# A block mask made from a 24-column one-hot, and expert rows loaded sooner, in a fused attention and mixture-of-experts kernel

## The chip, the cores and the metric

The kernel runs on one core of one Trainium2 chip. Its time is device microseconds, and before the change the median of 3 runs was 718.14 us (717.37 to 718.94). The core has five engines that run side by side, each through its own list of instructions in order, and wait for each other by semaphores: TensorE (PE, matrix products; PEld is its loading of weights), VectorE (DVE), ScalarE (ACT), GpSimd (POOL) and SyncE (SP, which here only issues transfers). An instruction that waits holds up everything behind it on its own engine.

## The reference

Block-sparse attention (BigBird's mask) over 4 batches, 8 heads, 768 positions and 64 dimensions is followed by a mixture of 8 experts, to each of which a token is sent by the cosine of its row with the expert's embedding. Cut to what matters here:

```python
mask = np.abs(blk_i - blk_j) <= 1                       # blocks of 32 positions, 24 of them
mask = mask | (blk_i == 0) | (blk_j == 0) | (blk_i == 23) | (blk_j == 23)
for qb in range(24):
    for kb in sampled_blocks[qb]:                       # 3 random blocks for each
        mask[qb*32:(qb+1)*32, kb*32:(kb+1)*32] = True
scores = np.where(mask, q @ k.T / 8, -1e9)
attn = softmax(scores) @ v                              # for each batch and head
x = heads side by side                                  # 3072 tokens of 512
xn, en = x / |x|, expert_emb / |expert_emb|
expert = argmax(xn @ en.T / tau); gate = softmax(...)[expert]
out[token] = gate * (relu(x[token] @ w1[expert]) @ w2[expert])
```

## The kernel before

The mask is added inside the score products. A key in block n has a one-hot row `kmask` (1 in row n), a query has a column `qmask` (0 where its block may see block n, -1e9 where not), and the product of the two, accumulated into the same PSUM tile as q·k, masks the scores. `kmask` and `qmask` are built once, at the start, from the 24x24 block mask `m`:

```python
def block_mask(k, exact=False):
    dif = iota(k, "dif", [NB, NB], [[1, NB]], mult=-1)          # column - row, on POOL
    col = iota(...); row = iota(...)
    m = dif * dif;  m = m <= 1.5                                # DVE, 24x24
    for val in (0.0, float(NB - 1)):
        for pos in (col, row):
            ins = nc.vector.scalar_tensor_tensor(out=m, in0=pos, scalar=val, in1=m, op0=ALU.is_equal, op1=ALU.max)
    with k.tc.issue_after(ins.ins):
        nc.vector.tensor_copy(out=ids_f, in_=k.ids[:, :, 0])    # the sampled blocks
    for r in range(NRAND):
        nc.vector.scalar_tensor_tensor(out=m, in0=col, scalar=ids_f[:, r:r + 1], in1=m, op0=ALU.is_equal, op1=ALU.max)
    nc.gpsimd.memset(both, 0.0)
    ins = nc.vector.tensor_scalar(out=both[:, :, 0:NB], in0=m..., scalar1=1.0, scalar2=-NEG, ...)
    k.mask_rows = ins.ins
    return both

def build_mask(k):
    nc.vector.memset(k.kmask[0:D], 1.0)                         # 64 x 768
    both = block_mask(k)
    one = k.kmask[0:D]
    nc.gpsimd.affine_select(out=one, in_=one, pattern=[[1, S]], compare_op=ALU.is_ge, fill=0.0, base=0, channel_multiplier=-BLK)
    nc.gpsimd.affine_select(out=one, in_=one, pattern=[[-1, S]], compare_op=ALU.is_ge, fill=0.0, base=BLK - 1, channel_multiplier=BLK)
    nc.scalar.copy(out=k.kmask[D:P], in_=k.kmask[0:D])          # the second head's 64 rows
    ps = k.big.tile([P, 2, 512], F32, name="qr", tag="big")
    for i in range(2):                                          # spread the mask over 768 queries
        cols = slice(i * HALF, (i + 1) * HALF)
        nc.tensor.matmul(ps[:, i, 0:HALF], lhsT=both..., rhs=k.kmask[0:NB, cols], start=True, stop=True)
    for i, copy in enumerate((nc.vector.tensor_copy, nc.scalar.copy)):
        k.masked.append(copy(out=k.qmask[:, cols of half i], in_=ps[:, i, 0:HALF]).ins)
```

The queries and keys of the first pair of heads come as two halves (`part` 0 and 1), are turned by DVE in 32x32 blocks (`kt`, `qt`), and then a unit of work is 128 keys against 384 queries for two heads. There are 192 units, 12 for a pair of heads. Each is scored, exponentiated by ACT, summed by DVE (`esum`), and multiplied with v (`av`). After every six units `av` is copied to `at`, and a few units later `settle` sends it back through TensorE (`back`), with the normed expert rows as further columns, which needs `build_experts` to be done.

```python
def warm_up(k, times):                                          # products of zeros
    ...
    ps = k.acc.tile([P, 2, 512], F32, name="warm", tag="av")
    for i in range(times):
        k.nc.tensor.matmul(ps[:, 0], lhsT=k.zeros[:, 0:P], rhs=k.zeros, start=True, stop=True)

def build_experts(k):                                           # a generator: yields cut it into steps
    nc.scalar.activation(sq, emb, ACT.Square, accum_out=nrm)
    nc.gpsimd.tensor_tensor(out=nrm, in0=nrm, in1=k.half[0:E, 0:1], op=ALU.pow)
    ...; yield
    nrm = (nrm + 1e-6) * tau; nrm = 1 / nrm; emb = emb * nrm     # three DVE operations
    yield
    for c in range(ND):
        nc.tensor.transpose(tp[:, c * E:(c + 1) * E], emb[:, c * P:(c + 1) * P], k.ident[0:E, 0:E])
    ...; yield

def attention_fast(n, ctx):
    load_ids(n); load_blocks(n, 0, 0); load_pair(n, 0, (2,)); load_blocks(n, 0, 1)
    warm_up(n, 8)
    build_mask(n)
    for part, behind in enumerate((n.mask_rows, n.masked[0])):
        with n.tc.issue_after(behind):
            for i in range(2):
                turn_blocks(n, 0, i, part)
    build_ident(n); score_fast(n, 0); score_fast(n, 1); build_consts(n)
    load_blocks(n, 1)                                           # the next pair's k and q
    load_pair(n, 1, (2,))                                       # its v
    load_experts(n)                                             # expert rows and tau
    for u in range(units):
        ...
        if u in (2, 4, 7): next(experts)                        # a step of build_experts
        steps = [attend_fast(u), score_fast(u + 2)]             # the other way round at the first of six units
```

The score products, the mask first (`score_fast`):

```python
    for rows, cols, first in ((k.kmask, k.qmask, True), (kt, qt, False)):
        for h, r, keys in quarters:
            nc.tensor.matmul(ps[D * r:D * (r + 1), h, 0:HALF], lhsT=rows[D * h:D * (h + 1), keys],
                             rhs=cols[D * h:D * (h + 1), queries], start=first, stop=not first)
    k.exps = nc.scalar.activation(e, ps[:, :, 0:HALF], ACT.Exp, scale=SCALE)
```

The score tiles and the spread share two PSUM buffers (`big`), `av` and the warm-up tile one (`acc`). The instructions are ordered by a scheduler when the program is built, and `issue_after` keeps one behind another on its engine. The second half of the kernel, the experts' products, is not touched by the change.

## Time and profile before

| | before |
|---|---|
| median of 3 runs | 718.14 us |
| span of the profiled run | 719.4 us |
| TensorE busy | 698.3 us (97%), 8308 products |
| DVE busy | 335.0 us (47%) |
| GpSimd busy | 229.0 us (32%) |
| ACT busy | 188.5 us (26%) |

Attention takes about the first half of the span and the experts the second. The page divides the span into 40 slices and gives for each the busy tenths of every engine and the clock that TensorE was granted, in tenths of full speed. The chain of waits, followed back from the last instruction, lies 87% on TensorE and 4% on DVE. In the lists of groups and in the timeline, a line gives the start and length in us, the engine, the line of the kernel, the operation, the tiles it writes and reads with their shape, and in square brackets how long its engine had been idle before it and who ended that. PE intervals are modelled, so a busy TensorE need not be at its peak.

### The profile page before, as it was taken

How to read it: one execution, taken by the hardware profiler on the slowest of the kernel's cores; microseconds unless marked ns; L12 is line 12 of the kernel's file. 1: busy time of each engine (PE TensorE's matmuls, PEld its weight loads, DVE VectorE, ACT ScalarE, POOL GpSimd, SP SyncE). 2: the span in 40 equal slices, each digit the busy share in tenths (PEclk: the TensorE clock that was granted, in tenths of full speed). 3: DMA queues.
4: the chain of work that ended last, by engine and by line, in shares of the span. 5: the costliest groups of instructions: out<-in, count | busy, mean ns of one | idle time of the engine just before them, and what ended most of it. 6: DMA issues, size and time to landing. Idle time of an engine off the chain costs nothing.

```text
span 719.4 us, 19421 instructions
## 1 busy us (share of the span) xinstructions
PE 698.3 (97%) x8308; PEld 447.8 (62%) x8308; DVE 335.0 (47%) x683; ACT 188.5 (26%) x266; POOL 229.0 (32%) x385
## 2 busy tenths in 40 slices
PE   7899999999999999999999999999999999999992
PEld 3585555555555455556777677766576665767771
DVE  6677778777788888776582111111111111111110
ACT  4355554454545544554100000000000000000000
POOL 2225547554754547653601111111111121111110
PEclk9899999999999999999999999999999999999997
DMA  6433333365335947642999998998899998999980
GB/s 111 91 67 69 69 68 68 64 154 113 52 69 126 181 99 224 201 136 82 328 316 400 397 337 325 342 338 303 297 396 398 398 347 305 404 397 401 340 321 23
DMA packets 180808, 164.76 MB, mean 229 GB/s; under 512 B 128284, under 2 KB 128284, under 8 KB 180710
## 3 DMA queue, kind: packets, MB, share of 16 engines
q1 hardware_dynamic: 174950, 149.80, 66.6%
q0 software_dynamic: 4160, 13.39, 4.7%
q8 instruction: 69, 1.13, 0.7%
q10 hardware_dynamic: 1600, 0.20, 0.2%
q14 instruction: 29, 0.24, 0.1%
HBM read 147.62 MB, written 16.01 MB: 227 GB/s over the span
## 4 chain that ended last, share of the span: by engine, by line
PE 87%; DVE 4%; issue 3%; POOL 1%; DMA 1%; ACT 1%; SPq 1%; DVEq 0%; POOLq 0%; ACTq 0%
PE hp L840 21%; PE yp L853 21%; PE sc L353 19%; PE av L374 16%; PE back L409 3%; PE hp L881 2%; PE yp L901 2%; PE back L402 1%; PE xg_ps L825 1%; ACT e L356 1%; DVE kt L269 1%; DVE esum L371 1%; DVE at L380 0%; DMA out_dram<-y,slot_l 0%; DMA kld<-in_k_dram 0%
## 5 line engine op out<-in xcount | busy, mean ns | idle before, releaser
L356 ACT ACTIVATE e<-sc 128x768 f32<-128x768 f32 x192 | 155.7, 811 | 161.5 <-PE sc L353 156.3
L840 PEld LDWEIGHTS hp<-xgt,w 128*128 128x128 f32 x1472 | 167.7, 192 | 10.8 <-issue 10.2
L840 PE MATMUL hp<-xgt,w 128*128 128x128 f32 x1472 | 169.1, 275 | 0.0
L353 PE MATMUL sc<-qt,kt 64*64 64x384 f32 x1536 | 167.6, 489 | 0.0
L374 PE MATMUL av<-e,vld 64*64 64x384 f32 x1536 | 162.1, 491 | 2.3 <-DVE at L380 2.0
L853 PE MATMUL yp<-w,h 128*128 128x512 f32 x368 | 162.0, 593 | 0.1
L371 DVE TENSOR_TENSOR esum<-esum,e 128x768 f32<-128x768 f32 x128 | 130.9, 1023 | 44.0 <-ACT e L356 42.2
L853 PEld LDWEIGHTS yp<-w,h 128*128 128x128 f32 x368 | 68.0, 190 | 77.5 <-issue 76.3
L437 POOL TENSOR_TENSOR sq<-sq 128x192 f32<-128x192 f32 (+1 forms) x186 | 103.2, 555 | 13.9
L862 POOL DMA_INDIRECT out_dram<-y,slot_l x20 | 20.2, 1009 | 246.0 <-DVE y L861 233.9
L374 PEld LDWEIGHTS av<-e,vld 64*64 64x64 f32 x1536 | 58.6, 134 | 58.7 <-issue 26.7
L843 ACT ACTIVATE h<-hp 128x512 f32<-128x512 f32 x23 | 13.7, 597 | 298.3 <-PE hp L840 284.4
L353 PEld LDWEIGHTS sc<-qt,kt 64*64 64x64 f32 x1536 | 64.7, 135 | 37.3 <-issue 34.2
L861 DVE TENSOR_SCALAR y<-yp,xg 128x512 f32<-128x512 f32 x25 | 18.8, 750 | 140.7 <-PE yp L853 128.2
L847 DVE TENSOR_SCALAR h<-hp 128x512 f32<-128x512 f32 x23 | 15.9, 691 | 131.3 <-PE hp L840 131.3
L353 PE MATMUL sc<-qmask,kmask 64*64 64x384 bf16 x768 | 71.6, 327 | 1.0 <-DVE qmask L167 1.0
L433 POOL TENSOR_TENSOR sq<-x 128x384 f32<-128x384 f32 x31 | 27.0, 873 | 121.7 <-DVE part L422 108.5
L353 PEld LDWEIGHTS <-kmask 64*64 64x64 bf16 x768 | 27.9, 108 | 32.2 <-issue 31.3
L369 DVE TENSOR_TENSOR esum<-e 128x768 f32<-128x768 f32 x32 | 31.1, 973 | 11.5 <-ACT e L356 10.8
L409 PE MATMUL back<-ones,esum 64*64 64x1 f32 x1536 | 27.5, 192 | 0.0
L409 PEld LDWEIGHTS back<-ones,esum 64*64 64x64 f32 x1536 | 26.6, 137 | 0.0
L780 POOL DMA_INDIRECT xg<-x_dram,slot_l x22 | 22.6, 1026 | 6.7 <-issue 6.7
(193 smaller groups left out, 364.1 us busy)
## 6 DMA issues: line engine op xcount, KB each, us to landing
w<-in_moe_w_dram SPq DMA_DIRECT2D x54, 2048.0 KB
w<-in_moe_w_dram SPq DMA_DIRECT2D x16, 512.0 KB
x_dram<-x SPq DMA_DIRECT2D x24, 256.5 KB
vld<-in_v_dram SPq DMA_DIRECT2D x32, 192.0 KB
kld<-in_k_dram SPq DMA_DIRECT2D x60, 96.0 KB
qld<-in_q_dram SPq DMA_DIRECT2D x60, 96.0 KB
x_early<-x SPq DMA_DIRECT2D x12, 256.5 KB
ticks<-dens SPq DMA_DIRECT2D x32, 0.0 KB
```

The costliest lines, as they stand in the source:

```text
L353: nc.tensor.matmul(ps[D * r:D * (r + 1), h, 0:HALF], lhsT=rows[D * h:D * (h + 1), keys], rhs=cols[D * h:D * (h + 1), queries], start=first ...
L356: k.exps = nc.scalar.activation(e, ps[:, :, 0:HALF], ACT.Exp, scale=SCALE)
L369: k.summed = nc.vector.tensor_tensor(out=k.esum, in0=k.first, in1=e, op=ALU.add)
L371: k.summed = nc.vector.tensor_tensor(out=k.esum, in0=k.esum, in1=e, op=ALU.add)
L374: nc.tensor.matmul(k.av[D * h:D * (h + 1), r, 0:HALF], lhsT=v[D * r:D * (r + 1), h, kc, :], rhs=e[D * r:D * (r + 1), h, :], start=(kc == 0 ...
L409: nc.tensor.matmul(sums[D * s:D * (s + 1), t, h, r:r + 1], lhsT=esum[D * r:D * (r + 1), h, cols], rhs=k.ones[D * r:D * (r + 1), 0:1], star ...
L433: nc.gpsimd.tensor_tensor(out=sq, in0=x, in1=x, op=ALU.mult)
L437: k.squared = nc.gpsimd.tensor_tensor(out=out, in0=sq[:, :, 0:width], in1=sq[:, :, width:2 * width], op=ALU.add).ins
L780: k.nc.gpsimd.indirect_dma_start(out=x[:, :], out_offset=None, in_=(k.x_dram if late else k.x_early)[:, :], in_offset=bass.IndirectOffsetO ...
L840: nc.tensor.matmul(hp[:, f, :], lhsT=w1[:, d, (f0 + f) * P:(f0 + f + 1) * P], rhs=xt[:, d, :], start=(d == 0), stop=(d == ND - 1))
L853: nc.tensor.matmul(yp, lhsT=h[:, f, :], rhs=w2[:, f, :], start=(f == 0), stop=(f == NF - 1))
L862: nc.gpsimd.indirect_dma_start(out=k.out[:, :], out_offset=bass.IndirectOffsetOnAxis(ap=slot, axis=0), in_=y[:, :], in_offset=None, bounds ...
```

## The change

The one-hot rows of `kmask` repeat each block's column 32 times. The change makes them in 24 columns (`hot`, 128x24) with two small DVE comparisons, and lets the readers repeat each column by a stride of zero: ACT's copy into `kmask`, now for both heads at once, and the two products that spread the mask over the queries. The 64x768 memset and the two 64x768 selects are not needed then. The two halves of `qmask` are copied apart: the first by ACT, the second by DVE, behind the turns of the first halves of k and q. Five more products of zeros are placed between the spread and the first scores, to keep TensorE at work there. The expert rows and tau are loaded ahead of the second pair's blocks and not behind them, so that `build_experts` can be ordered sooner.

```diff
@@ warm_up
-    ps = k.acc.tile([P, 2, 512], F32, name="warm", tag="av")
+        k.warm = k.acc.tile([P, 2, 512], F32, name="warm", tag="av")     # made once, with the zeros
     for i in range(times):
-        k.nc.tensor.matmul(ps[:, 0], ...)
+        k.nc.tensor.matmul(k.warm[:, 0], ...)
@@ block_mask
-    dif = iota(k, "dif", [NB, NB], [[1, NB]], mult=-1)
+    lanes = iota(k, "dif", [P, NB], [[1, NB]], mult=-1)
+    dif = lanes[0:NB]
...
+        k.hot = pool.tile([P, NB], BF16, name="hot")
+        for h in range(2):
+            rows = slice(D * h, D * (h + 1))
+            ins = nc.vector.tensor_scalar(out=k.hot[rows], in0=lanes[rows], scalar1=-float(D * h), scalar2=None,
+                                          op0=ALU.is_equal)
@@ build_mask
-    nc.vector.memset(k.kmask[0:D], 1.0)
-    one = k.kmask[0:D]
-    nc.gpsimd.affine_select(...)                                         # twice
-    nc.scalar.copy(out=k.kmask[D:P], in_=k.kmask[0:D])
+    nc.scalar.copy(out=k.kmask.rearrange("p (n t) -> p n t", t=BLK), in_=k.hot.unsqueeze(2).broadcast_to([P, NB, BLK]))
     for i in range(2):
-        nc.tensor.matmul(ps[:, i, 0:HALF], lhsT=both..., rhs=k.kmask[0:NB, cols], ...)
+        some = k.hot[0:NB, i * (NB // 2):(i + 1) * (NB // 2)]
+        k.spread = nc.tensor.matmul(k.qr[:, i, 0:HALF], lhsT=both...,
+                                    rhs=some.unsqueeze(2).broadcast_to([NB, NB // 2, BLK]), start=True, stop=True).ins
-    for i, copy in enumerate((nc.vector.tensor_copy, nc.scalar.copy)): ...
+    mask_half(k, 0, nc.scalar.copy)
@@ attention_fast
     build_mask(n)
-    for part, behind in enumerate((n.mask_rows, n.masked[0])):
-        with n.tc.issue_after(behind):
+    with n.tc.issue_after(n.spread):
+        warm_up(n, 5)
+    for part in range(2):
+        with n.tc.issue_after(n.masked[1] if part else n.mask_rows):
             for i in range(2):
                 turn_blocks(n, 0, i, part)
+        if part == 0:
+            with n.tc.issue_after(n.turns):
+                mask_half(n, 1, n.nc.vector.tensor_copy)
...
+    load_experts(n)
     load_blocks(n, 1)
     load_pair(n, 1, (2,))
-    load_experts(n)
```

As built, the order of the engines changes only at the start: the steps of `build_experts` come on ACT behind the exponential of unit 3 (before: of unit 9), and the four small transposes of the expert rows on TensorE lie between the attention products of units 6 and 7 (before: among the scores of unit 10).

## The prediction

> **What bounds the kernel now.** I read the table of engines first: TensorE is busy for 698.3 of 719.4 us. Then the granted clock by stretch, which I cut at the places where the clock changes:
>
> ```profile
> 0.00:10.83 10.83, 7.05 (x38) 3.05 (x42) 6.97 (x23) 3.40 (x4) 4.24 (x20) 0.84 0.67 118
> 10.83:24.48 13.65, 13.37 (x180) 6.64 (x172) 10.52 (x16) 8.20 (x12) 0.00 (x0) 1.00 0.76 139
> 24.48:27.90 3.42, 1.42 (x32) 0.97 (x34) 1.83 (x7) 0.23 (x2) 0.75 (x1) 1.00 0.73 117
> 27.90:34.72 6.82, 6.82 (x104) 5.65 (x100) 3.12 (x7) 1.46 (x2) 3.40 (x7) 0.50 0.02 5
> 34.72:300.00 265.28, 263.29 (x5042) 151.94 (x5038) 209.73 (x414) 137.23 (x187) 143.73 (x254) 1.00 0.50 105
> ```
>
> After the stretch and its length, the columns are PE, weight loads, DVE, ACT, POOL, clock, DMA share, GB/s. From 34.72 us on TensorE is never free for long and its clock is full. So only the first 35 us can give anything, and what they give should arrive whole at the end: the later weight loads are triggered by work that moves with it. Two places stand out: the opening, with a half clock from 7.41 to 10.83, and 24.48 to 34.72, where TensorE idles and then runs 6.82 us at 0.50.
>
> The timeline of the opening, by engine, shows why scores begin at 7.52:
>
> ```profile
> 1.30 0.70 DVE L152 MEMSET kmask<- 64x768 bf16 x1
> 2.06 0.88 DVE L127 TENSOR_SCALAR m<-m 24x24 f32<-24x24 f32 x1
> 2.08 0.85 POOL L155 TENSOR_SCALAR_AFFINE_SELECT kmask<-kmask 64x768 bf16<-64x768 bf16 x1 [0.67 <-DVE m L126]
> 3.05 0.82 POOL L157 TENSOR_SCALAR_AFFINE_SELECT kmask<-kmask 64x768 bf16<-64x768 bf16 x1
> 3.07 0.83 DVE L130 SCALAR_TENSOR_TENSOR m<-col,m 24x24 f32<-24x24 f32 x1
> 4.00 0.17 DVE L130 SCALAR_TENSOR_TENSOR m<-row,m 24x24 f32<-24x24 f32 x1
> ...
> 5.78 0.17 DVE L140 TENSOR_SCALAR both<-m 24x48 bf16<-24x48 f32 x1
> 5.98 0.58 DVE L269 STREAM_TRANSPOSE kt<-kld 128x384 f32<-128x384 f32 x1
> 6.49 0.54 DVE L269 STREAM_TRANSPOSE qt<-qld 128x384 f32<-128x384 f32 x1
> 6.95 0.52 DVE L167 CAST qmask<-qr 128x384 bf16<-128x384 f32 x1
> 7.50 0.48 ACT L167 CAST qmask<-qr 128x384 bf16<-128x384 f32 x1 [2.57 <-DVE qmask L167]
> 7.52 0.54 PE L353 MATMUL sc<-qmask,kmask 64*64 64x384 bf16 x4 [1.01 <-DVE qmask L167]
> ```
>
> The same 24x24 operation takes 0.83 us beside an affine_select of POOL and 0.17 us afterwards. The DVE chain memset, mask, two transposes, copy is what ends last. The eight warm-up products end at 4.49; TensorE then works 0.49 us until 7.52, and the first 24 score products run in 3.46 us.
>
> The chain of the expert rows, from the timeline around 24 us:
>
> ```profile
> 23.84 0.61 ACT L214 ACTIVATE emb_sq<-emb 8x512 f32<-8x512 f32 x1
> 24.37 0.18 ACT L214 ACTIVATION_READ_ACCUMULATOR emb_sq<-emb 8x1 f32 x1
> 24.64 0.75 POOL L215 TENSOR_TENSOR emb_nrm<-emb_nrm,half 8x1 f32<-8x1 f32 x1 [19.00 <-ACT emb_sq L214]
> 25.42 0.20 DVE L220 TENSOR_SCALAR emb_nrm<-emb_nrm,tau 8x1 f32<-8x1 f32 x1 [0.48 <-DMA qld<-in_q_dram]
> 25.66 0.15 DVE L221 RECIPROCAL emb_nrm<-emb_nrm 8x1 f32<-8x1 f32 x1
> 25.90 0.47 DVE L222 TENSOR_SCALAR emb<-emb,emb_nrm 8x512 f32<-8x512 f32 x1
> 26.52 0.38 PE L226 MATMUL tp<-ident,emb 8*128 8x8 f32 x4 [2.00 <-DVE emb L222]
> ```
>
> The bracket of the last line is the reading: TensorE stood for 2.00 us because the transposes of the expert rows lie in its order in the middle of unit 10's scores, while ACT, POOL and DVE were only then making them.
>
> [...] the changes stand at 7.41, 10.83, 27.90 and 34.72, multiples of 3.41 apart, and each half-clock stretch follows a window in which TensorE was mostly idle (4.00 to 7.41; 24.48 to 27.90, busy 1.42 of 3.42). [...] the trace's copy of kmask took 0.83 us with 64 lanes, so my estimate for the new copy over 128 lanes is the same 0.83.
>
> **The change, part by part.**
>
> (a) One-hot. Out go the 0.70 us memset and both POOL selects; in come two DVE operations on 64x24. The largest like them, `both`, took 0.17, so 0.1 to 0.17 each. The DVE order of the changed kernel is zeros, m, hot twice, m, ids_f, four m, three m, both. It starts when the iota is there (1.07, so about 1.25) instead of 1.92, and loses the two blocked operations (0.88 and 0.83 become about 0.17 each). It is at ids_f by about 1.8, which now precedes the four L130 operations and must wait for the ids transfer; the trace's landings have it complete at 2.21. From the start of the second L130 operation to the end of `both` the old trace has 4.00 to 5.95 = 1.95; plus 0.2 for the first, 2.15. So `both` ends near 2.25 + 2.15 = 4.4, at worst 4.7 if the two 128x128 selects of POOL (0.29 and 0.31) still hit it. Before: 5.95. Gain 1.3 to 1.5 us, but not all on the path:
>
> (b) The transposes. The four k transfers of the first half are unchanged, and their last landing is at 5.25 in the old trace. So kt can start at 5.3 rather than 5.98, and qt ends near 6.4. Half of the gain of (a) is swallowed here.
>
> (c) The halves of the mask. Half 0 goes to ACT: table load to 4.08, kmask copy to 4.9, then the qmask copy of 0.48, about 5.5. It no longer stands behind the transposes on DVE, where it cost 0.45 (7.02 to 7.47). Half 1 stays on DVE after the turns, ending near 7.0; unit 1 needs that only because its score buffer is the one that held the spread, and unit 1 comes at about 7.3. So the first q·k products can start at 6.45 instead of 7.79.
>
> (d) Warm-up. Five more products after the spread (about 4.5 to 5.0). The old ones follow each other at 0.43 us before 4.00, at half clock; at full clock I take 0.21, so 1.07 in all, ending near 6.1, before qt. The window 4.00 to 7.41 is then almost fully busy and the next one should be at full clock. The first 24 score products took 3.46 us at 0.50; the later units do 12 in 1.19 (0.35 + 0.84), so 24 in about 2.4. Unit 2's scores end near 9.4 instead of 11.74: 2.3 us earlier.
>
> (e) What is left of this at the next gate. DVE must copy `at` of the first half before unit 6 can attend: old start 20.13. Now the expert chain comes before: esum of unit 3 near 12.1 to 13.1, POOL's power to about 13.65, then 0.97 for the three expert operations, two esum, two kt transposes (1.03), the back copies (0.55): `at` starts near 18.2, TensorE resumes near 18.8 instead of 20.74. It would have been ready at about 17.8, so it idles about 1 us. **Gain carried: 1.9 us.**
>
> (f) Expert rows. Their load is issued at about 8.7 instead of 17.85, ahead of pair 1's blocks, so it lands near 11.5 if it takes the old 2.75 (17.85 to the last landing at 20.60). ACT squares them after unit 3, and the transposes on TensorE are placed in unit 6's attention (about 19 us), 4 us after the rows are ready. **2.0 us of idle go**, and with them the half clock: 6.82 us at 0.50 did the work of 3.41 at 1.00, **3.4 us more**. Pair 1's k blocks are issued about 0.4 us later (9.5 instead of 9.11) and are read only at about 16.7: no cost.
>
> Sum: 1.9 + 2.0 + 3.4 = 7.3. A cross-check: from `at` to `at` is 16.27 us for the first pair (20.13 to 36.40), and 10.24 for a later one (46.19 to 56.43), a surplus of 6.03, which with 1.9 makes 7.9. I take 7.7: 718.14 - 7.7 = 710.4.
>
> **Rivals.** First, loads bind the opening: (b) is already that in part. If k's first half lands later than 5.25, or q's, the mask's gain vanishes and warm-up becomes filler; what remains is the clock of (d). For it: DVE waited 0.49 us on kld at 8.51 for the second half. Total gain then near 6.5, time 711.6. Second, the warm-up itself delays: if the window's phase leaves the five products at half clock they take 2.15 us and end at 7.1, 0.7 after qt. Part of it is hidden behind (e)'s gate; 711 to 711.5. Third, DVE becomes the bound: the expert chain sits in front of esum, transposes and `at`, and DVE's wait for POOL is dead time. If `at` comes only at 19.5, the start's gain falls to 0.6 and the time is about 711.8; if the idle also makes a cold window, 713.5. Fourth, the cold stretch at 28 us is due to the many one-column products of the first `back` (1.6 us of them there), not to the idle. Against it: later pairs have the same products at clock 1.00 up to 300 us. If it held, only 2.0 + 1.9 would come: 714.2.
>
> **Range and chances.** All four rivals end between 710 and 714.2, and none makes the kernel slower: everything added is 1.07 us of TensorE in otherwise idle time and two short DVE operations. A surplus of 0.5 us over the cross-check gives 709.7; runs of before scatter by 1.6. So 708.7 to 713.3. Two per cent faster would be 703.8, which takes twice the sum; 2% slower has no source.
>
> **What would show it.** Right: POOL without 64x768 selects, `both` done by 4.7; first q·k products at 6.3 to 6.6, granted clock 1.00 from 4.0 through 40; `at` at 18 to 18.5 with an idle of about 1 us before unit 6; no wait of `tp` on DVE; second `at` near 28.3 instead of 36.40. Wrong: a half-clock stretch anywhere in 7 to 40 us, an idle over 2 us before unit 6, or a first product later than 7.

## The result, and the profile after

| | before | after |
|---|---|---|
| median of 6 runs each, side by side | 719.13 us (717.37 to 719.61) | 712.15 us (711.12 to 713.08) |
| ratio, with its 95% interval | 1 | 0.9907 (0.9893 to 0.9922) |
| span of the profiled run | 719.4 us | 711.0 us |
| mean granted clock of TensorE | 0.987 | 0.994 |
| TensorE busy | 698.3 us | 693.6 us |

The kernel became faster: the two medians lie 6.98 us apart, and the ratio makes the gain 0.93%, or 6.7 us. The mean clock of 0.994 still holds the last 8.5 us of the span (from 702.5), which are at 0.50 and in which TensorE has nothing to do; what lay before the first clock record of the trace is counted in it as full clock. The prediction was 710.4 us, with a range from 708.7 to 713.3.

First the windows of the kernel after, with the columns as before: PE, weight loads, DVE, ACT and POOL busy (with counts), clock, DMA share, GB/s.

```profile
2.85:6.26 3.41, 3.41 (x9) 0.86 (x8) 2.29 (x9) 2.54 (x3) 0.47 (x1) 1.00 1.07 204
...
7.06:19.39 12.33, 11.53 (x158) 6.04 (x157) 8.80 (x17) 8.07 (x12) 0.75 (x1) 1.00 0.82 146
19.39:30.00 10.61, 10.61 (x200) 5.92 (x204) 8.55 (x18) 4.64 (x8) 2.94 (x5) 1.00 0.58 94
30.00:40.00 10.00, 10.00 (x200) 5.65 (x196) 8.44 (x15) 5.45 (x8) 4.95 (x8) 1.00 0.62 108
```

From 19.39 us on TensorE is busy in every hundredth of the window, at clock 1.00. Neither the idle 2.00 us nor the half-clock stretch of 6.82 us is there any more. Only the first row misleads: the clock column shows 1.00 until the trace has its first clock record, and that record comes at 6.26 in this run. What ran before it is told by the products themselves.

The timeline of the opening, by engine (start, length, engine, line, operation, tiles; in brackets the idle time before it and who ended it):

```profile
1.20 0.57 DVE L137 TENSOR_SCALAR hot<-dif 64x24 bf16<-64x24 f32 x2
1.25 3.60 PE L80 MATMUL warm<-zeros 128*128 128x512 bf16 x8 [1.25 <-DVE zeros L77]
...
4.14 0.18 DVE L148 TENSOR_SCALAR both<-m 24x48 bf16<-24x48 f32 x1
4.78 0.82 PE L165 MATMUL qr<-hot,both 24*128 24x384 bf16 x2
5.17 0.58 DVE L274 STREAM_TRANSPOSE kt<-kld 128x384 f32<-128x384 f32 x1 [0.86 <-DMA kld<-in_k_dram]
5.53 1.59 PE L80 MATMUL warm<-zeros 128*128 128x512 bf16 x5
5.64 0.48 ACT L172 CAST qmask<-qr 128x384 bf16<-128x384 f32 x1 [0.71 <-PE qr L165]
5.68 0.54 DVE L274 STREAM_TRANSPOSE qt<-qld 128x384 f32<-128x384 f32 x1
...
7.06 0.36 PE L358 MATMUL sc<-qmask,kmask 64*64 64x384 bf16 x4
7.24 0.81 PE L358 MATMUL sc<-qt,kt 64*64 64x384 f32 x8
```

The mask rows are ready at 4.32 instead of 5.95, and the transposes are then held by the landing of k (0.86 us of DVE waiting on a DMA). But the first score product waits for neither of them: `qt` is done at 6.22, the mask's first half at 6.12, and TensorE goes on with its products of zeros until about 7.1. Three things add up there, all before the full clock came at 6.26. The eight products of zeros ran at half clock (3.60 us, 0.45 each) and ended at 4.85, so that the spread began at 4.78, 0.46 us after the mask rows were ready; the two spread products took 0.82; and the five products took 1.59, since the first two of them began before 6.26 as well. A later run of the same kernel, shown below, has 0.50 for the spread and 1.25 for the five, 0.25 each, at full clock.

The expert rows in the timeline of the kernel after, and the two `at` copies that the prediction names:

```profile
12.87 0.61 ACT L219 ACTIVATE emb_sq<-emb 8x512 f32<-8x512 f32 x1
...
14.92 0.47 DVE L227 TENSOR_SCALAR emb<-emb,emb_nrm 8x512 f32<-8x512 f32 x1
18.77 0.56 DVE L385 TENSOR_TENSOR at<-av,part 128x384 f32<-128x384 f32 x1
19.39 0.88 PE L379 MATMUL av<-e,vld 64*64 64x384 f32 x8 [0.67 <-DVE at L385]
20.19 0.41 PE L231 MATMUL tp<-ident,emb 8*128 8x8 f32 x4
...
28.93 0.56 DVE L385 TENSOR_TENSOR at<-av,part 128x384 f32<-128x384 f32 x1 [0.56 <-ACT part L383]
```

The rows are normed at 15.39 and turned at 20.19, without a wait: the row of `tp` has no bracket. The second `at` starts at 28.93 instead of 36.40. The same two copies in the kernel before:

```profile
20.13 0.56 DVE L380 TENSOR_TENSOR at<-av,part 128x384 f32<-128x384 f32 x1
36.40 0.56 DVE L380 TENSOR_TENSOR at<-av,part 128x384 f32<-128x384 f32 x1 [1.96 <-ACT part L378]
```

The wait that is gone was not one for the transfer itself. In the kernel before the rows had landed at 20.60, and ACT took them up at 23.84 only, because their square stood behind the exponential of unit 9 in its order. The place of the load in the program decided the place of this work. Whether moving the work alone, with the load where it was, would have been enough wasn't tried.

So the two profiled runs differ as follows. The first `at` comes 1.36 us sooner (20.13 to 18.77). From the first to the second the kernel needs 10.16 us instead of 16.27, which is 6.11 less. From the second to the third it needs 9.79 in both. The rest of the span is 673.21 us before and 672.28 after, 0.93 less. This last part isn't the change: over the fourteen profiles of this study it lies between 671.4 and 673.2, whatever the kernel.

### The profile page after: what moved, and what is told of

Read it like the earlier page. It is cut to its first block, busy times and chain, and to the rows that moved or that the text cites. A ratio compares the mean times of both kernels' runs of the same rounds, so it can differ in the third digit from the quotient of the medians.

```text
span 711.0 us, 19426 instructions
## 1 busy us (share of the span) xinstructions
PE 693.6 (98%) x8313; PEld 436.5 (61%) x8313; DVE 332.6 (47%) x684; ACT 188.5 (27%) x266; POOL 230.0 (32%) x383
## 4 chain that ended last, share of the span: by engine, by line
PE 90%; issue 3%; DVE 3%; POOL 1%; ACT 1%; DMA 1%; POOLq 0%; DVEq 0%; SPq 0%; ACTq 0%
PE hp L845 21%; PE yp L858 21%; PE sc L358 20%; PE av L379 17%; PE back L414 3%; PE hp L886 2%; PE yp L906 2%; PE xg_ps L830 1%; PE back L407 1%; ACT e L361 1%; PE warm L80 1%; DVE kt L274 1%; DVE esum L376 1%; DVE at L385 0%; DMA out_dram<-y,slot_l 0%
## 5 line engine op out<-in xcount | busy, mean ns | idle before, releaser
L358 PE MATMUL sc<-qt,kt 64*64 64x384 f32 x1536 | 157.9, 482 | 0.0
L379 PE MATMUL av<-e,vld 64*64 64x384 f32 x1536 | 154.9, 487 | 3.0 <-DVE at L385 2.8
L442 POOL TENSOR_TENSOR sq<-sq 128x192 f32<-128x192 f32 (+1 forms) x186 | 106.0, 570 | 13.9
L379 PEld LDWEIGHTS av<-e,vld 64*64 64x64 f32 x1536 | 53.8, 133 | 61.0 <-issue 28.2
L358 PEld LDWEIGHTS sc<-qt,kt 64*64 64x64 f32 x1536 | 58.9, 133 | 38.5 <-issue 36.2
L358 PE MATMUL sc<-qmask,kmask 64*64 64x384 bf16 x768 | 65.9, 323 | 0.1
L358 PEld LDWEIGHTS <-kmask 64*64 64x64 bf16 x768 | 24.7, 107 | 33.1 <-issue 33.0
```

The costliest lines, as they stand in the source:

```text
L379: nc.tensor.matmul(k.av[D * h:D * (h + 1), r, 0:HALF], lhsT=v[D * r:D * (r + 1), h, kc, :], rhs=e[D * r:D * (r + 1), h, :], start=(kc == 0 ...
L442: k.squared = nc.gpsimd.tensor_tensor(out=out, in0=sq[:, :, 0:width], in1=sq[:, :, width:2 * width], op=ALU.add).ins
```

## The experiments

The theory is that two separate things were removed. The wait of the expert transposes cost its own 2.00 us and, through the clock, up to 3.4 us more; and the opening cost a window at half clock and a late start. A window is here a stretch of 3.41 us: the changes of the clock in the profile of before (7.41, 10.83, 27.90 and 34.72) lie multiples of it apart. The rivals were these: the half clock after the wait comes from the many one-column products behind it; the opening's gain comes from the mask being ready and not from the clock; and the 0.67 us of idle that is left before unit 6 hides a further gain. "Ratio" is always the time over that of the kernel before in the same comparison, with its 95% interval.

| run | edit | median, us | ratio |
|---|---|---|---|
| b_experts_first | before, expert rows loaded sooner | 715.57 | 0.9944 (0.9932 to 0.9957) |
| a_experts_last | after, expert rows loaded last again | 717.39 | 0.998 (0.9969 to 0.9991) |
| b_filled | before, transposes gathered, 9 products of zeros in their wait | 719.49 | 0.9998 (0.998 to 1.0017) |
| b_unfilled | the same without the 9 products | 719.69 | 1.0009 (0.9999 to 1.0018) |
| a_last_filled | a_experts_last with the 9 products | 714.87 | 0.9943 (0.9929 to 0.9958) |
| a_no_warm | after without the five extra products | 711.57 | 0.9896 (0.9879 to 0.9914) |
| a_selects_dead | after, with the memset and both selects on a dead tile | 712.76 | 0.9918 (0.9898 to 0.9939) |
| a_at_first | after, `at` ahead of other work on DVE | 712.06 | 0.9905 (0.9889 to 0.9921) |
| a_chain | a_at_first, and one pair of turns later | 711.55 | 0.9903 (0.9888 to 0.9918) |
| after_again | after, unchanged | 711.70 | 0.991 (0.9897 to 0.9924) |
| b_warm | before, with the five products only | 716.94 | 0.9979 (0.9962 to 0.9996) |
| b_filled_again | b_filled, unchanged | 718.51 | one run |

### One part at a time

**b_experts_first.** The kernel before, with one of the change's edits:

```diff
+    load_experts(n)
     load_blocks(n, 1)
     load_pair(n, 1, (2,))
-    load_experts(n)
```

> The kernel before, with the load of the expert rows moved ahead of the second pair's blocks and nothing else. Theory (the expert rows carry most of the gain, by the idle and by the half clock behind it): the stretch from the first at to the second goes from 16.27 us to about 10.2, no half clock between 24 and 40 us, and against that the expert chain of DVE comes ahead of the first at and delays it by up to 0.9 us, so 5.2 to 6.1 us less than before, ratio 0.9915 to 0.993. The opening stays: half clock there, first scores at 7.5. Rival (the clock falls because of the one-column products of the first back): only the idle goes, 2 us less, ratio 0.997, and a half-clock stretch remains near 28 us.

Measured: 715.57 us, 0.9944. Two rows of TensorE's timeline, and the window of the first scores:

```profile
21.19 0.88 PE L374 MATMUL av<-e,vld 64*64 64x384 f32 x8 [0.66 <-DVE at L380]
22.00 0.41 PE L226 MATMUL tp<-ident,emb 8*128 8x8 f32 x4
```

```profile
8.74:12.16 3.42, 3.42 (x28) 1.73 (x24) 0.96 (x1) 2.19 (x3) 0.00 (x0) 0.50 0.71 116
```

The transposes wait for nothing, the clock stays full behind them, and the first `at` and the second are 10.12 us apart. The opening still has its 3.42 us at half clock, with 28 products in them; rows of windows at full clock further down have 51 and 52. The load's place alone thus removes everything that happened at 24 to 35 us. Of the time it brings 4.0 us in the medians, less than the 5.2 to 6.1 expected from the profile of before: that profile is of a run of 721.16 us, 3 us above the first median of before, so it shows more of this loss than the usual run has.

**a_experts_last.** The kernel after, with that same edit taken back.

```diff
-    load_experts(n)
     load_blocks(n, 1)
     load_pair(n, 1, (2,))
+    load_experts(n)
```

> The changed kernel with the expert rows loaded where they were, behind the second pair's blocks: the mask, the apart copies and the five products alone. Theory: the opening keeps its gain, and the first at comes sooner than in the changed kernel because DVE has no expert chain before it, at about 18.0 instead of 18.77 (20.13 in the kernel before). The idle of 2 us before the expert transposes comes back, and behind it half clock for one or two windows of 3.4 us. Time 2 to 2.3 us less than before, ratio 0.997. Rival (the opening carries as much as the expert rows): ratio 0.994 or less. Rival (the opening's gain is lost in a longer wait at the expert transposes, whose rows come by a chain that does not depend on the mask): ratio 0.999 to 1.000.

Measured: 717.39 us, 0.998. Its windows around the transposes, and their row:

```profile
21.30:24.72 3.42, 1.42 (x14) 0.52 (x10) 2.16 (x7) 0.60 (x2) 0.75 (x1) 1.00 0.92 146
24.72:31.55 6.83, 6.83 (x111) 4.99 (x112) 2.83 (x8) 1.62 (x2) 2.66 (x6) 0.50 0.01 3
31.55:34.96 3.41, 3.41 (x51) 2.19 (x47) 1.81 (x4) 2.29 (x4) 0.93 (x3) 1.00 0.28 64
```

```profile
23.86 0.38 PE L231 MATMUL tp<-ident,emb 8*128 8x8 f32 x4 [2.00 <-DVE emb L227]
```

The whole pattern of the kernel before is back: the 2.00 us wait, then two windows at half clock. Only the first of the two follows the wait. The second follows a window (24.72 to 28.13) in which TensorE was busy throughout, with 84 products of which 72 are the small ones of `back`, and the clock stayed at half all the same; in the kernel before it is likewise (27.90 to 31.31, busy throughout with 80 products). So the early mask and the warm-up don't protect what comes later, and most of the change's gain hangs on the place of one load. In the medians the load is worth 0.73% on top of the other parts (0.998 to 0.9907), about 5.2 us, and the other parts are worth 0.37% on top of the load (0.9944 to 0.9907), about 2.7 us; these ratios come from two comparisons, each with its own runs of the kernel before. Alone they brought 4.0 and 1.4 us, together 6.7. The difference between 5.4 and 6.7 is within the combined uncertainty of the three ratios (0.22%, or 1.6 us), so that the parts help each other isn't shown.

### Is it the idle, or the products behind it?

**b_filled** and **b_unfilled.** The kernel before, with the expert transposes moved behind the whole of unit 10's scores, and then with nine products of zeros in front of them, into a bank that nobody reads. b_unfilled has the move without the products.

```diff
-    tp = two_banks(k, "tp")[:, 0]
+    tps = two_banks(k, "tp")
+    tp = tps[:, 0]
+    for i in range(9):                      # b_unfilled: range(0)
+        nc.tensor.matmul(tps[:, 1], lhsT=k.zeros[:, 0:P], rhs=k.zeros, start=True, stop=True)
...
-        if u in (2, 4, 7):
+        if u in (2, 4):
...
+        if u == 8:                          # behind the scores of unit 10
+            with n.tc.issue_after(n.scored.ins), n.tc.issue_after(n.summed.ins), n.tc.issue_after(n.exps.ins):
+                next(experts)
```

> The kernel before, with the expert transposes behind unit 10's scores and nine products of zeros put just ahead of them, so that TensorE works through the time in which it waited for the expert rows. The wait itself stays as long. Theory (the half clock comes from the idle): clock 1.00 from 11 us on, and 3.4 us less than the same kernel without the nine products. Rival (it comes from the one-column products of the first back, or from the end of the warm-up): half clock near 28 us as before, and the same time within 0.3%.

> The control of the run with nine products of zeros: the same kernel without them. Both theories: the wait of about 2 us and the half clock behind it as in the kernel before, ratio 0.998 to 1.002.

Measured: 719.49 and 719.69 us, both as the kernel before within their intervals. The 3.4 us that the filling was expected to bring did not show in the medians, and by them alone filling the wait seemed useless. The profiles say otherwise for the run that each shows. The profiled run of b_filled (717.57 us) is at full clock from 11.1 us on, with 0.50 us of the wait left. That of b_unfilled (719.76 us) waits 2.55 us and has this in its windows:

```profile
23.65:27.07 3.42, 1.64 (x24) 0.63 (x16) 2.88 (x8) 2.23 (x4) 1.30 (x1) 1.00 0.50 79
27.07:30.48 3.41, 2.64 (x87) 2.18 (x91) 2.27 (x8) 0.00 (x0) 0.00 (x0) 1.00 0.55 91
30.48:33.89 3.41, 3.41 (x31) 2.56 (x26) 1.17 (x5) 0.81 (x1) 2.10 (x4) 0.50 0.00 0
```

The window with the most idle (1.64 busy of 3.42) was followed by a window at full clock. The next one, busy for 2.64 us, was followed by half clock. What differs is what ran in it: 0.77 us of idle and 87 products, of which 48 are the one-column products of the first `back`; the earlier one holds products of 384 columns and nothing else. So busy time alone didn't decide the clock here, and the prediction's fourth rival, which put the half clock down to those products, had a piece of the truth.

The twelve runs of b_filled fall into two groups, five from 716.5 to 717.9 and seven from 719.4 to 720.8 us, 2.7 us apart by their medians. A window of 3.41 us at 0.50 loses 1.7 us of work (an estimate from these two figures), so this would fit one or two windows that are lost in some runs and kept in others.

**b_filled_again.** The same kernel.

> One more look at the kernel before with nine products of zeros ahead of the expert transposes: its runs fell into two heaps, near 717 and near 720, and the profile was of the first. Theory (phase of the clock windows): where the opening stays at half clock until 13 us, the nine products are not to blame, and the time of the second heap shows as a half-clock stretch besides, of 3.4 us or more, in a window that holds the rest of the wait, the expert transposes and the first back. Rival: the products themselves run at half clock and end after the wait, so that they cost time.

Measured: one run, 718.51 us. Its windows, which begin 0.8 us later on the program than those of b_filled:

```profile
22.11:25.53 3.42, 3.26 (x34) 1.52 (x28) 2.91 (x7) 2.22 (x4) 1.30 (x1) 1.00 0.53 79
25.53:28.94 3.41, 2.90 (x81) 1.77 (x81) 2.14 (x7) 0.00 (x0) 0.00 (x0) 1.00 0.66 106
28.94:32.35 3.41, 3.41 (x37) 2.78 (x37) 1.21 (x5) 0.01 (x1) 1.64 (x3) 0.50 0.00 0
```

Here the 0.50 us that is left of the wait and the one-column products lie in the same window, and the next is at half clock. In b_filled the wait lay in the window 24.75 to 28.16 and nearly all the one-column products in the next, and neither of the two was followed by half clock. The zeros themselves ran at full clock (eight recorded in 1.89 us, 0.24 each, where those of the opening took 0.45 at half clock in the kernel after), so the rival of this run, that they run at half clock themselves, is refuted. The second `at` comes 1.68 us later than in b_filled (35.08 against 33.40), which is that one window. So in these two profiles it hung on where the windows fell on the program, 0.8 us apart, whether this kernel lost a window. What divides the other runs into two groups is likely of this kind, but it isn't shown: this run, at 718.51, lies between the groups, and only two of the thirteen runs have a profile.

**a_last_filled.** The same filling in a_experts_last, where the opening is that of the kernel after. Edit: the nine products of b_filled and the transposes behind unit 10's scores.

> The changed kernel with the expert rows loaded last again, and nine products of zeros ahead of the expert transposes, which stand behind unit 10's scores. It is the earlier pair of runs (with and without nine products) on a kernel whose opening is at full clock more often; compare with the run of the expert rows last (ratio 0.998). Theory (the idle brings the half clock): clock 1.00 from the opening on, the wait as long as before but filled, 2 to 3.4 us less, ratio 0.9935 to 0.995. Rival (the products cost as much as they save, or half clock comes anyway): ratio 0.997 to 0.999.

Measured: 714.87 us, 0.9943 against 0.998 without the filling. Two rows of TensorE's timeline, and the windows:

```profile
22.11 2.12 PE L232 MATMUL tp<-zeros 128*128 128x512 bf16 x9
24.78 0.38 PE L234 MATMUL tp<-ident,emb 8*128 8x8 f32 x4 [0.55 <-DVE emb L227]
```

```profile
23.17:26.58 3.41, 2.85 (x47) 1.46 (x49) 2.17 (x8) 0.00 (x0) 0.48 (x1) 1.00 0.68 108
26.58:30.00 3.42, 3.42 (x89) 2.87 (x85) 1.42 (x6) 0.81 (x1) 1.29 (x2) 1.00 0.02 5
```

TensorE works no sooner on anything useful. It only multiplies zeros where it idled, and the kernel is faster by 0.37%, 2.7 us. The 6.83 us at half clock are gone. This is the theory's own test: with the idle filled the half clock is gone, so the clock is a loss besides the wait. One thing is not separated: the edit also moves the transposes behind unit 10's scores. On the kernel before that move alone brought nothing (b_unfilled, 1.0009); on this kernel it wasn't run alone. The step from here to the kernel after, 0.9943 to 0.9907 or 2.6 us, is then what the wait itself cost; in this profile it is 2.12 us of zeros and 0.55 of idle, 2.67 together.

### The opening: mask, warm-up or phase?

**a_no_warm.** The kernel after, without the five products.

```diff
-    with n.tc.issue_after(n.spread):
-        warm_up(n, 5)
```

> The changed kernel without the five products between the spread and the first scores. Theory (they fill time in which TensorE has nothing to do, and in the profiled run they were granted half clock, so that they end 0.8 us after qt is ready): first scores at 6.2 to 6.3 instead of 7.06, the first at up to 0.8 us sooner, and 0.3 to 0.8 us less than the changed kernel where the clock window is kind; where it is not, the first scores run at half clock and 1 to 2 us are lost. On the median between 0.5 us less and 1 us more, ratio to before 0.990 to 0.992, with a wider scatter than the changed kernel's 2 us. Rival (they earn what they were put there for): 1.5 us or more above the changed kernel, ratio 0.9925 or more.

Measured: 711.57 us, but the four runs are 711.47, 711.52, 711.62 and 714.33. The profile is of the last. Its first scores in TensorE's timeline, and the windows:

```profile
6.17 0.54 PE L358 MATMUL sc<-qmask,kmask 64*64 64x384 bf16 x4 [0.57 <-ACT qmask L172]
6.44 1.54 PE L358 MATMUL sc<-qt,kt 64*64 64x384 f32 x8
```

```profile
3.43:6.85 3.42, 2.85 (x14) 1.01 (x16) 2.44 (x10) 1.96 (x3) 0.00 (x0) 1.00 1.06 201
6.85:10.26 3.41, 3.41 (x28) 1.66 (x24) 0.95 (x6) 1.43 (x2) 0.00 (x0) 1.00 0.51 84
10.26:13.67 3.41, 3.41 (x52) 1.90 (x48) 2.40 (x3) 1.72 (x4) 0.00 (x0) 1.00 0.73 120
```

The first clock record is at 10.26, so again the column shows nothing before it, and the products do: 28 in the window from 6.85, 52 in the next. Without the warm-up the first scores start 0.9 us sooner and run at half clock for 4.1 us. The window from 3.43 was busy for 2.85 of 3.42 us and didn't bring the full clock; it held the end of the first warm-up, the spread, whose products are over 24 rows (24*128 in the timeline), an idle 0.57 and the first scores. The five products may thus be an insurance: three of the four runs without them are 0.1 to 0.7 us faster than the medians of the kernel after (711.5 to 711.6 against 712.15 and 711.70, from different comparisons), and this one is 2.2 to 2.6 us slower. But only this one run has a profile, and its windows fall later (one ends at 6.85) than those of any profile with the five products and the change's opening (the latest at 6.36), so that the products would have brought the full clock here isn't shown. On the mean of these few runs (712.2 without, 712.2 and 711.8 with) neither is better.

**a_selects_dead.** The kernel after, with the work that the change took out put back on a tile that nobody reads.

```diff
+    dead = pool.tile([P, S], BF16, name="dead")
+    nc.vector.memset(dead[0:D], 1.0)
     both = block_mask(k)
+    one = dead[0:D]
+    nc.gpsimd.affine_select(out=one, in_=one, pattern=[[1, S]], ...)
+    nc.gpsimd.affine_select(out=one, in_=one, pattern=[[-1, S]], ...)
```

> The changed kernel with the old memset and the two 64x768 selects put back as dead work: they write a tile that nothing reads. Theory (they block DVE, and that is what the one-hot of 24 columns saves): the two DVE operations beside the selects take 0.8 us again, the mask rows are done 1.3 to 1.8 us later, near 5.7 instead of 4.3; of that 0.5 to 1.3 us reach the first scores, since the transposes of k wait for their load until 5.2 and lie behind the mask rows on DVE; ratio to before 0.991 to 0.9925. Rival (the selects are harmless beside other work): the same as the changed kernel, and the DVE operations at 0.2 us.

Measured: 712.76 us, 0.9918. The timeline of DVE and POOL, and TensorE's first rows:

```profile
1.96 0.97 DVE L137 TENSOR_SCALAR hot<-dif 64x24 bf16<-64x24 f32 x2
2.07 0.82 POOL L164 TENSOR_SCALAR_AFFINE_SELECT dead<-dead 64x768 bf16<-64x768 bf16 x1 [0.67 <-DVE m L127]
3.02 0.85 POOL L166 TENSOR_SCALAR_AFFINE_SELECT dead<-dead 64x768 bf16<-64x768 bf16 x1
3.24 0.67 DVE L131 SCALAR_TENSOR_TENSOR m<-col,m 24x24 f32<-24x24 f32 x1
...
5.57 0.17 DVE L148 TENSOR_SCALAR both<-m 24x48 bf16<-24x48 f32 x1
...
6.24 1.25 PE L80 MATMUL warm<-zeros 128*128 128x512 bf16 x5
...
7.60 0.81 PE L365 MATMUL sc<-qt,kt 64*64 64x384 f32 x8
```

Two small operations end with the two selects of POOL (2.93 beside 2.89 and 3.91 beside 3.87 us), and both began after the select beside them: one of 0.67 us where its like take 0.17, and the second of the pair `hot`, which took 0.80 us where the first took 0.15. By what means a select holds an operation of DVE isn't shown. `both` ends at 5.74, 1.4 us later than in the kernel after.

What this costs depends on the clock of the opening. In this profile the first full clock comes at 4.60, and in the profile of the kernel after that is nearest to it (after_again, below) at 4.12. Between these two the first q·k product moves from 6.28 to 7.60 and the second `at` from 27.97 to 29.29: 1.32 us, nearly the whole delay of the mask rows. About 0.2 of it may be the later clock (an estimate from a_at_first, where the full clock came at 5.67 and the first q·k product at 6.95). Beside the first profile of the kernel after, which was at half clock until 6.26, only 0.36 us are left (7.24 to 7.60), because there the products of zeros held the scores back anyway. In the medians the kernel loses 0.6 to 1.1 us by the selects (712.76 against 712.15 and 711.70, from different comparisons), and the ratios 0.9918 and 0.9907 aren't told apart. So the early mask can be worth about 1.1 us, and how much of it the usual run keeps isn't shown.

**b_warm.** The kernel before, with the five products behind its spread and nothing else.

```diff
+    with n.tc.issue_after(n.spread):
+        warm_up(n, 5)
```

> The kernel before with the five products between the spread and the first scores, and nothing else. Theory (the warm-up is worth something by keeping the opening at full clock, and it needs the time between spread and scores): the products lie between 6.5 and 7.6 to 8.6, so that the scores start up to 1 us later than 7.52, but at full clock, which saves 1.7 us of the 3.4 at half; the first at 0.5 to 1.2 us sooner, and the two half-clock windows behind the expert rows stay. Ratio 0.998 to 0.9995. Rival (the opening was cold because of the long pause before the spread, 4.5 to 6.0, which five products behind it don't fill): the half clock stays, the scores start later, ratio 1.000 to 1.002.

Measured: 716.94 us, 0.9979, over 17 runs from 714.8 to 721.7. In the profiled run the five took 2.31 us at half clock, the first score came at 8.99 instead of 7.52, and yet the span is 3.8 us shorter than that of before, 3.3 of it between the first `at` and the second, where there is no half clock after the 2.00 us wait:

```profile
23.66:27.08 3.42, 1.53 (x20) 0.48 (x12) 2.36 (x6) 1.41 (x3) 0.75 (x1) 1.00 0.65 106
27.08:30.49 3.41, 3.30 (x100) 2.75 (x104) 1.74 (x6) 0.81 (x1) 0.00 (x0) 1.00 0.25 39
30.49:33.90 3.41, 3.41 (x52) 2.83 (x48) 2.09 (x6) 1.99 (x3) 2.35 (x3) 1.00 0.02 5
```

The same wait cost a_experts_last two windows at half clock and this run none. In the window of the wait TensorE has 1.53 us of products of 384 columns here; there it had 1.42 us, of which the four transposes, over 8 rows, are 0.38. The one-column products come in the next window here, which has hardly any idle. So this kernel, with the old place of the load, got off lightly in this run, likely by where its windows fell, and its 17 runs scatter over 7 us. That is not what was expected: the half clock behind the expert rows was to stay and the first `at` to come sooner. It came at 20.80, 0.67 us later than in the profile of before, so in this run the five products brought nothing in the opening, and where the 0.2% of the median comes from stays open.

**after_again.** The kernel after, once more, to see what its profile is in another run.

> The changed kernel once more, beside the others on one chip. 711.5 to 712.7 us, ratio 0.990 to 0.9915. Its clock windows will lie elsewhere; if the five products do what they are for, the first scores run at full clock at this phase too, and start between 6.2 and 7.1.

Measured: 711.70 us in five runs (710.95 to 713.0). The profiled one has its first full clock at 4.12 instead of 6.26:

```profile
4.49 0.50 PE L165 MATMUL qr<-hot,both 24*128 24x384 bf16 x2
4.91 1.25 PE L80 MATMUL warm<-zeros 128*128 128x512 bf16 x5
...
6.10 0.36 PE L358 MATMUL sc<-qmask,kmask 64*64 64x384 bf16 x4
6.28 0.81 PE L358 MATMUL sc<-qt,kt 64*64 64x384 f32 x8
```

The same rows as in the first profile, at full clock: the first q·k product at 6.28 instead of 7.24, and the first two `at` at 17.81 and 27.97 instead of 18.77 and 28.93. The 0.96 us are kept to the second `at`, and the span is 709.2.

### Is there more to be had?

**a_at_first.** In the kernel after TensorE still stands for 0.67 us before unit 6, until DVE has copied `at` behind two transposes of the next keys and other work. Here `at` is first in DVE's order, and the expert steps come later.

```diff
-        if u in (2, 4, 7):
+        if u in (2, 6, 8):                  # the later two behind at, not behind esum
...
-            with n.tc.issue_after(n.summed.ins):
+            with n.tc.issue_after(n.summed.ins if g else n.ats.ins):
                 turn_blocks(n, g + 1, turn)
```

> The changed kernel, with the copy of the first at put on DVE ahead of the second pair's k transposes, of the expert rows' three operations and of the back copies, and the expert transposes behind unit 10's scores. Theory (the first at gates unit 6's attention and took 0.67 us of idle and some 0.6 us more behind DVE's expert chain): at at 17.6 to 17.8 instead of 18.77, 0.7 to 1.3 us less than the changed kernel, ratio to before 0.989. Rival (DVE only moves its work, and TensorE waits for it later, at the expert transposes or at the exponentials that wait for esum): the same as the changed kernel within 0.3 us.

Measured: 712.06 us, as the kernel after. The profile has the idle before unit 6 gone (`at` at 17.44) and a new one in TensorE's order:

```profile
23.43 0.65 PE L407 MATMUL back<-back,at 64*64 64x72 f32 x22 [0.96 <-DVE back L239]
```

The copies that `back` reads are now the last of DVE's queue. The wait has moved some five microseconds on; the second `at` is at 29.02, where it was at 28.93. Counted from the first q·k product, which takes the clock of the opening out of the comparison, it comes after 22.07 us here and after 21.69 in both profiles of the kernel after.

**a_chain.** In addition the second pair's `q` turns go behind those copies.

```diff
-        turn = u % per - (0 if g else NC - 1)
+        turn = u % per if g else {NC - 1: 0, NC + 2: 1}.get(u, -1)
...
-            with n.tc.issue_after(n.summed.ins if g else n.ats.ins):
+            with n.tc.issue_after((n.summed if g else n.backed if turn else n.ats).ins):
```

> The changed kernel with the first at ahead on DVE, as in the run before, and the second pair's q transposes put behind the last copies of the expert rows. Theory (in that run the wait only moved: TensorE stood 0.96 us before the first back, for copies that lay behind 1.03 us of transposes): the first back starts near 22.7 instead of 23.43, the second at near 28.2 instead of 28.9 to 29.0, and 0.7 to 1.3 us less than the changed kernel, ratio to before 0.989. Rival (it moves once more, to the scores of unit 12, which read those q transposes): the same as the changed kernel within 0.3 us, with a new idle near 26 us.

Measured: 711.55 us (711.01 to 712.2), beside 711.70 of the kernel after in the same comparison. In its profile TensorE is idle for 0.20 us in all from 1.25 to 60 us. The second `at` comes at 28.44 in a run whose first full clock is at 6.36, half a microsecond before the first profile of the kernel after, and 21.15 us after the first q·k product. In the medians nothing can be told apart: the 0.7 to 1.3 us expected of each of these two runs did not come. So no version clearly beats the changed kernel, and what freeing DVE's order brought in these first 30 us is 0.5 us or less.

## Why the prediction was right, step by step

**Steps (a) and (b) held.** `both` ends at 4.32 (predicted 4.4), `kt` starts at 5.17 (5.3) behind k's landing, `qt` ends at 6.22 (6.4). The first rival, that loads bind, is right to the extent that step (b) had already said. Step (a) took the two long operations of DVE as held by the selects, and a_selects_dead shows the like again (0.67 us where 0.17 is usual). Which of the two begins first didn't decide it: of the pair 0.88 beside 0.85 DVE begins 0.01 us before the select and is still the one held, and of the pair 0.83 beside 0.82 it begins 0.02 us after.

**Step (c) held, its consequence didn't.** ACT's half of the mask is ready at 6.12 instead of 5.5, because the eight products ahead of the spread and the spread itself ran at half clock (in after_again it is ready at 5.50), and the first q·k product comes at 7.24 instead of 6.45. That was on the list of what would show the prediction wrong ("a first product later than 7" — it was 7.06).

**Step (d) is the term that was mis-sized.** It took the five products at full clock, 1.07 us ending near 6.1. They took 1.59 and ended near 7.1, 0.84 us after `qt`. This is the second rival, which put the end at 7.1 and 0.7 after `qt`; that it hit the end is partly luck, since it had all five at half clock (2.15 us) from about 5.0, and they began at 5.53 with only the first two of them at half clock. The prediction chose between them by the clock windows of one profile, and the windows begin elsewhere in other runs (first full clock at 6.26 us in after, at 4.12 in after_again): in after_again the five took 1.25, and the opening was a little ahead of the prediction's numbers (6.28 for the first q·k product, `at` at 17.81 and 27.97, predicted 6.45, 18.2 and 28.3). The purpose of the step held in both: no half clock in the first scores.

**Step (e) carried 1.36 us and not 1.9** in the first profile, and 2.32 in the second (20.13 to 17.81). The start of this difference moves just as much: in the other profiles with the old opening and the expert rows last the first `at` is at 19.61, 19.62, 20.80 (b_warm) and 20.83. The idle before unit 6 is 0.67 us, not 1.0. The third rival, DVE as the bound, is refuted as a loss: freeing `at` of it moved the wait (a_at_first), and freeing `back` as well brought 0.5 us in one profile and nothing that the medians show (a_chain).

**Step (f) held.** Predicted were 5.4 us as a sum and 6.0 by the cross-check from `at` to `at`; the profiled pair shows 6.11. The first pair now takes 10.16 us where a later pair took 10.24. The two terms of the sum were separated by runs: 2.7 us for the clock (a_experts_last to a_last_filled), predicted 3.4, and 2.6 us for the wait (a_last_filled to after), predicted 2.0. Each of these differences is uncertain by 1.3 us or more. Of the 6.11 us, 1.66 is less idle between the two copies (2.28 before, 0.62 after) and 3.41 is the half clock's (an estimate: half of 6.82 us at 0.50). The remaining 1.0 is neither: in b_warm, which had the wait and no half clock, TensorE is busy for 10.67 us between the two copies, and in the kernel after for 9.54, with the same numbers of products but for one. A third of it is where the count begins (at the first `at` of before TensorE still has 0.33 us of unit 7's scores to do, in the kernel after none); the rest goes with the transposes' place among the scores of unit 10. The sum of step (f) left this out, and the cross-check from `at` to `at` held it without naming it. The fourth rival is refuted as it was put, since the same one-column products are at full clock in the kernel after, but true in part: a wait of 0.5 us in the same window with them was followed by half clock (b_filled_again), and the second of the two half-clock windows follows one that they filled, and no idle (a_experts_last). The prediction's reading that each half-clock stretch follows a mostly idle window holds in the profile of before for the first window of a stretch only, and in b_unfilled and b_filled_again not for that one either (the windows ahead of it were busy for 2.64 and 2.90 of 3.41 us).

**The sum** was 7.3 us and the cross-check 7.9; 7.7 was taken between them, and 7.0 were measured in the medians. The error of the time, 1.75 us, has two parts. 0.99 is the start: before was 718.14 us in the three runs that were known and 719.13 in six. 0.76 is the gain, and of that step (e) makes 0.54 in the profiled run. That the number came so close owes something to luck: the part of step (f) that the sum lacked and the part of step (e) that it had too much are of opposite sign. That the two profiled spans differ by 8.4 us, more than the medians, is because the known profile of before was of a run (721.16 us) above all six of these; a sum read from one profile takes that run's bad luck with it.

**Open:** how often the windows fall badly. The first full clock was seen at 4.12 to 6.36 us in the seven profiles of kernels with the change's own opening and its five products, and none of these had half clock in the scores of units 0 to 2; all five profiles with the old opening and no extra products had a window of it there, and so had a_no_warm, without the five products, and b_warm, with them behind the old opening (until 10.01). That is a count of profiles, and it doesn't give the share of runs.

## What to carry to other kernels

When TensorE is busy for 97% of the span, a short wait of it is worth reading together with the clock in the windows behind it: here 2.00 us of waiting for work on a small load that was issued last, and that was ordered late for it, cost about as much again in clock (2.6 and 2.7 us in the medians), and moving one line brought most of the gain. Read the order in which the queue issues the loads, and the place of the work on them in each engine's list, against the order in which they are needed, before shortening any operation. And take a profile twice before sizing a loss of a few microseconds in the first 40 us: the two profiles of the kernel after differ there by 0.96 us at the second `at`, with the first full clock at 6.26 us in one and at 4.12 in the other.

## What the runs showed of the hardware that was not expected

- The granted clock didn't go by busy time alone. A window of 3.42 us with 1.53 or 1.64 us of products of 384 columns was followed by full clock (b_warm, b_unfilled), and one that was busy for 2.64 or 2.90 us, in which 46 or more products had a single column, was followed by half clock (b_unfilled, b_filled_again). One at half clock that was busy for all of its 3.41 us, 72 of its 84 products being those of `back`, didn't bring the full clock back (a_experts_last). One with 2.85 us, partly of products over 24 rows, was followed by a window with 28 products where the next had 52 (a_no_warm). The windows began elsewhere in each of the two profiles of one kernel (first full clock at 6.26 and at 4.12 us, after and after_again).
- A wait of 2.00 us was followed by 6.83 us at half clock, or by none (a_experts_last, b_warm).
- The kernel before, in 59 runs side by side with the first experiments, lies between 716.5 and 721.3 us; the kernel after, in 11 runs, between 710.95 and 713.08. That the kernel after is steadier isn't shown by this: in the six runs of each side by side the two spread over 2.2 and 2.0 us.
- The pair of comparisons on 64x24 took 0.57 us (0.38 and 0.18), although no select of 64x768 was there, where the prediction had allowed 0.1 to 0.17 for each; POOL's small operations ran beside it, and whether they are the cause wasn't tried. It cost nothing, since the chain behind it waited for k.
